# Cached attention on one core: loads by four heads of a batch, K transposes on both sides of the scores, first q by three or four batch pairs

## The chip, the cores and the metric

The kernel runs on one core of a Trainium2 chip. The metric is the device time of one execution in microseconds (us). Before the change it is 869.04 us, the median of three runs (866.92 to 869.71).

## The reference

Two independent attention blocks, A and B, are computed and put side by side in the output. Each has 16 batches of 64 queries, 32 heads of 128 columns and a cache of 512 keys. All data are bf16.

```
q      = (x @ wq), split into heads            # x [16,64,640], wq [640,4096]
scores = q . k_cache * 128**-0.5               # [16,32,64,512]
p      = softmax(scores)
o      = p . v_cache                           # caches [16,32,512,128]
out    = o, heads joined, @ wo                 # wo [4096,640]
return concatenate([a, b], axis=-1)            # [16,64,1280]
```

The caches of both blocks together are 268 MB and are read once.

## The kernel before

**Tiles.** Two batches (a batch pair) fill the 128 rows of a tile: 64 queries of each. A step is one head of one batch pair: a score tile of 128 x 512, its softmax, its product with V. Two steps (two heads) are a macro step, numbered m; there are 256. Two macro steps, four heads, make a period; there are 128. A pass is one block with one half of the heads (16 heads, 8 batch pairs: 64 macro steps); there are four. Inside a pass the batch pairs follow one another, and the 16 heads within each.

**The work of one period on the tensor engine (PE).**

- KX: K arrives with keys on the partitions and is transposed by PE, 32 transposes of 64 rows for each macro step, into PSUM banks 6 and 7. KE on the vector engine (DVE) copies both banks to a slot of `ktp_ring`.
- SM: q times K transposed, the two batches in two column halves of the array. Four score tiles go to banks 2 to 5.
- MX (DVE) takes the row maximum, EX on the scalar engine (ACT) the exponential with its row sum, RC2 (DVE) the reciprocals of two steps, NM on POOL the division. NM also rearranges the columns of p, since K and V give the keys to partitions in different orders.
- TR2 transposes p on PE into banks 2 and 3, which the first two score tiles have left. TA2 (ACT, even m) and TE2 (DVE, odd m) copy it out. PV2 multiplies by V into bank 1, and OE4 (ACT) copies four heads of o out.
- OP2 multiplies o by the first 512 columns of wo, accumulating over the 16 heads in bank 0. OX does the other 128 columns once for every batch pair (16 matmuls, in bank 4, in one period of four). OVP and OXP keep the first half's sum; OVF and OXF add the second half and ST stores.
- QN computes q one half pass ahead, for one head and four batch pairs (five matmuls of 512 columns), into bank 1; QEN copies it to `qc_ring`. The first half pass has no QN before it: there QJ computes q of four heads for one batch pair, in each of the first 16 periods (20 matmuls of 128 columns), and QEJ copies it to `qj_ring`.

**What sets the order.** Every engine runs a list written out before the launch. The templates `PE_T`, `ACT_T`, `DVE_T`, `POOL_T` (lines 39 to 49) give, for a period, each operation, its offset in macro steps, and a time within 6.3 us; sorting by time gives the list. One template holds for the whole run. Dependences become semaphore waits, and redundant ones are pruned.

**Loads.** All loads are issued by SP, in one queue, in the order that `build_plan` computes: a load is due `LEAD` (K, V) or `WLEAD` (weights, x) macro steps before its first use, 9 in both cases, or when its ring slot comes free if that is later. A running clock `t_now`, advanced by `DMA_US` for each load, then ties each load to an instruction of PE: SP waits until PE has got there (`paced`). `STEP_US` says how long a macro step is taken to be.

- K: one load of 512 KB for each macro step, two heads of two batches, 2 KB for each partition and batch (line 702). `kn_ring` has 9 slots.
- V: two loads of 256 KB for each macro step, one for each batch, pieces of 1 KB (line 701). `v_ring` has 10 slots.
- wq and wo: 640 KB for four heads (lines 677 and 685).
- x: transposed by the DMA engines on the way in (line 691), four loads for block A (batch pairs 0; 4 to 7; 1; 2 and 3, in this order) and two for block B.

Of the kernel before, what the change touches and what calls it, by code (L numbers as in the profile page):

```python
# [15 lines left out]
class Cfg:  # L16
# [5 lines left out]
    NVB = 10  # L22
    LEAD = 9.0
    WLEAD = 9.0
    NQ = 2
    QLAG = 4
# [12 lines left out]
    PE_T = (("SM", 0, 0, 0.0), ("SM", 0, 1, 0.21), ("SM", 1, 0, 0.43), ("SM", 1, 1, 0.64), ("QJ", 2, 0, 0.72),  # L39
# [3 lines left out]
    ACT_T = (("OE4", -4, 0, 0.43), ("EX", 0, 0, 1.79), ("QEJ", 2, 0, 1.86), ("EX", 1, 0, 2.27), ("EX", 0, 1, 2.83),  # L43
             ("QEN", -2, 0, 3.25), ("TA2", -2, 0, 4.3), ("OVP", -3, 0, 4.75), ("ST", -9, 0, 5.02),
             ("EX", 1, 1, 5.55), ("OXP", -3, 0, 6.08))
    DVE_T = (("RC2", -1, 0, 0.31), ("MX", 0, 0, 1.61), ("MX", 1, 0, 2.12), ("MX", 0, 1, 2.28), ("KE", 2, 0, 2.3),
             ("MX", 1, 1, 2.91), ("RC2", 0, 0, 4.41), ("OVF", -3, 0, 5.09), ("OXF", -3, 0, 5.38),
             ("TE2", -1, 0, 5.72), ("KE", 3, 0, 5.87))
    POOL_T = (("NM", -1, 0, 1.99), ("NM", -1, 1, 4.17), ("NM", 0, 1, 4.44), ("NM", 0, 0, 5.74))
    ACT_TE = (0,)  # L50
    TRB = (0, 1)
    OXB = 2
    KFULL = ()


class Op:
# [3 lines left out]
    def __init__(self, eng, kind, idx, reads=(), writes=(), dur=0.0, ts=None, aux=None):  # L60
        self.eng = eng
        self.kind = kind
        self.idx = idx
        self.reads = tuple(reads)
        self.writes = tuple(writes)
        self.sem = None
        self.count = None
        self.deps = []
        self.waits = []
        self.early = None  # L70
        self.dur = dur
        self.ts = ts
        self.aux = aux
        self.dma = kind in ("LDK", "LDV", "LDX", "LDWQ", "LDWO", "ST")


def build_plan(dims, cfg):
# [41 lines left out]

    vectors = [tuple(QB * n + i for i in range(QB)) for n in range(HH + cfg.QLAG)]  # L120
    qvec, qcell = {}, {}
    for k in range(NPER):
        u, i, hc = k // PPQ, k % PPQ // HG, k % HG
        if k + PPQ < NPER:
            v = vectors.pop(0)
            qvec[k] = v
            for b in range(QB):
                qcell[u + 1, k % PPQ, b] = v[b]
        if u:
            vectors.append(tuple(sorted(qcell[u, G * hc + g, i] for g in range(G))))  # L130

    def qres(g):
        k, u = g // G, g // G // PPQ
        return ("qj", k % cfg.NQ) if u == 0 else ("qc", qcell[u, g % SPB, k % PPQ // HG])

    def trbank(m):
        return cfg.TRB[m % 2]

    def make_op(kind, m, sub, ts):
# [4 lines left out]
        if kind == "KX":  # L144
            return mk("pe", "KX", m, [("kn", m % cfg.NKB), ("ident",)], [("KTB",)], ts)
        if kind == "KE":
            return mk("dve", "KE", m, [], [("KTB",), ("ktp", m % cfg.NKT)], ts)
        if kind in ("MX", "EX", "NM"):
            g = 2 * m + sub
            r = g % cfg.NR  # L150
            if kind == "MX":
                return mk("dve", "MX", g, [], [("SB", g % cfg.NS), ("negmax", r)], ts)
            if kind == "EX":
                return mk("act", "EX", g, [("negmax", r)], [("SB", g % cfg.NS), ("p", g % cfg.NP), ("rowsum", r)], ts)
            return mk("pool", "NM", g, [("p", g % cfg.NP), ("recip", r)], [("pn", g % cfg.NPN)], ts)
        r0, r1 = g0 % cfg.NR, g1 % cfg.NR
        if kind in ("QJ", "QEJ"):
            if k >= PPQ:
                return None
            if kind == "QJ":  # L160
                return mk("pe", kind, k, [("xT", bp), ("wq", qslot(k % HG))], [("QOB",)], ts)
            return mk("act", kind, k, [], [("QOB",), ("qj", k % cfg.NQ)], ts)
        if kind in ("QN", "QEN"):
            if k not in qvec:
                return None
            u = k // PPQ + 1
            if kind == "QN":
                return mk("pe", kind, k, [("xT", u % 2 * QB + b) for b in range(QB)] + [("wq", qslot(k % PPQ // G))],
                          [("QOB",)], ts)
            return mk("act", kind, k, [], [("QOB",)] + [("qc", c_) for c_ in qvec[k]], ts)  # L170
        if kind == "SM":
            return mk("pe", "SM", (m, sub), [qres(2 * m + sub), ("ktp", m % cfg.NKT)], [("SB", (2 * m + sub) % cfg.NS)],
                      ts)
        if kind == "RC2":
            return mk("dve", "RC2", m, [("rowsum", r0), ("rowsum", r1)], [("recip", r0), ("recip", r1)], ts)
        if kind == "TR2":
            return mk("pe", "TR2", m, [("pn", g0 % cfg.NPN), ("pn", g1 % cfg.NPN), ("ident",)], [("SB", trbank(m))],
                      ts)
        if kind in ("TE2", "TA2"):
            if (kind == "TA2") != (m % 2 in cfg.ACT_TE):  # L180
                return None
            return mk("dve" if kind == "TE2" else "act", kind, m, [], [("SB", trbank(m)), ("pT", m % cfg.NT)], ts)
        if kind == "PV2":
            return mk("pe", "PV2", m, [("pT", m % cfg.NT), ("v", m % cfg.NVB)], [("QOB",)], ts)
        if kind == "OE4":
            return mk("act", "OE4", k, [], [("QOB",), ("oT", k % cfg.NO)], ts)
        if kind == "OP2":
            return mk("pe", "OP2", m, [("oT", k % cfg.NO), ("wo", wslot(ps_, h0 // G))], [("OUTB",)], ts)
        if h0 + 2 != SPB:
            return None  # L190
        lo = grp * MPG
        if kind == "OX":
            return mk("pe", "OX", m, [("oT", i % cfg.NO) for i in range(lo // 2, k + 1)]
                      + [("wo", wslot(ps_, i)) for i in range(HG)], [("SB", cfg.OXB)], ts, aux=(lo, m + 1))
        if kind in ("OVP", "OXP") and ps_ % NHALF == 0:
            return mk("act", kind, m, [], [("OUTB",) if kind == "OVP" else ("SB", cfg.OXB), ("outp", bp, kind[1])], ts,
                      aux=grp)
        if kind in ("OVF", "OXF") and ps_ % NHALF == 1:
            return mk("dve", kind, m, [("outp", bp, kind[1])],
                      [("OUTB",) if kind == "OVF" else ("SB", cfg.OXB), ("out_sb", kind[1])], ts, aux=grp)  # L200
# [4 lines left out]
    templates = {"pe": cfg.PE_T, "dve": cfg.DVE_T, "pool": cfg.POOL_T, "act": cfg.ACT_T}  # L205
    at = {}
    for eng, tmpl in templates.items():
        offs = [t[1] for t in tmpl]
        for k in range(-(max(offs) + 1) // 2 - 1, (NMAC - min(offs)) // 2 + 1):
            for kind, off, sub, t in tmpl:  # L210
                m = 2 * k + off
                if 0 <= m < NMAC:
                    op = make_op(kind, m, sub, 2 * k + 2 * t / cfg.PERIOD)
                    if op is not None:
                        progs[eng].append(op)
                        at[kind, m, sub] = op.ts

# [4 lines left out]
    NEG = -10 ** 9  # L222

    def add(ready, first, lead, rank, kind, idx, writes, aux):
        loads.append((max(ready, first - lead), first, rank,
                      mk("sp", kind, idx, [], writes, first - 0.01, aux=aux)))

    for ps_ in range(NPASS):
        for j in range(HG):
            first = at["QJ", j * MPC, 0] if ps_ == 0 else at["QN", (2 * ps_ - 1) * MPQ + j * MPG, 0]  # L230
            ready = NEG
            if ps_ == 1:
                ready = max(at["QN", j * MPG + MPG - 2, 0], at["QJ", MPQ - MPG + j * MPC, 0])
            elif ps_ > 1:
                ready = at["QN", (2 * ps_ - 2) * MPQ + j * MPG + MPG - 2, 0]
            add(ready, first, cfg.WLEAD, 0, "LDWQ", (ps_, j), [("wq", qslot(j))], (ps_, j))
            i = ps_ * HG + j
            ready = NEG
            if i >= cfg.NWO:
                ready = at["OX", ((i - cfg.NWO) // HG + 1) * MPP - 1, 0]  # L240
            first = at["OP2", ps_ * MPP + j * MPC, 0]
            add(ready, first, cfg.WLEAD, 3, "LDWO", (ps_, j), [("wo", wslot(ps_, j))], (ps_, j))

    for blk in range(NBLK):
        for lo, hi in ((0, 1), (4, 8), (1, 2), (2, 4)) if blk == 0 else ((0, 4), (4, 8)):
            q0 = lo // QB
            if blk:
                first = at["QN", (4 * blk + q0 - 1) * MPQ, 0]
                ready = at["QN", (4 * blk + q0 - 2) * MPQ - 2, 0]
            else:  # L250
                first = at["QN", 0, 0] if q0 else at["QJ", lo * MPG, 0]
                ready = NEG
            add(ready, first, cfg.WLEAD, -1, "LDX", (blk, lo), [("xT", bp) for bp in range(lo, hi)], (blk, lo, hi))

    for m in range(NMAC):
        for kind, ring, n_ring, cons, tb in (("LDK", "kn", cfg.NKB, "KX", 1), ("LDV", "v", cfg.NVB, "PV2", 2)):
            ready = at[cons, m - n_ring, 0] if m >= n_ring else NEG
# [546 lines left out]
```

## Time and profile before

| | us |
|---|---|
| median of three runs | 869.04 |
| profiled execution, its own time | 869.67 |
| its span, first to last instruction | 867.9 |
| PE busy | 832.1 |
| DVE busy | 730.7 |
| ACT busy | 638.0 |
| POOL busy | 418.7 |

The granted clock of the tensor engine is 0.998. The core read 289.41 MB and wrote 2.62 MB. Matmuls overlap in the pipeline, so their durations add to more than the time they take; the distance from one start to the next is the better measure. PEld is PE's weight load, which runs beside its matmuls. A wait marked `<-issue` has no semaphore behind it in the profile. [...]

### The profile page before, as it was taken

How to read it: one execution, taken by the hardware profiler on the slowest of the kernel's cores; microseconds unless marked ns; L12 is line 12 of the kernel's file. 1: busy time of each engine (PE TensorE's matmuls, PEld its weight loads, DVE VectorE, ACT ScalarE, POOL GpSimd, SP SyncE). 2: the span in 40 equal slices, each digit the busy share in tenths (PEclk: the TensorE clock that was granted, in tenths of full speed). 3: DMA queues.
4: the chain of work that ended last, by engine and by line, in shares of the span. 5: the costliest groups of instructions: out<-in, count | busy, mean ns of one | idle time of the engine just before them, and what ended most of it. 6: DMA issues, size and time to landing. Idle time of an engine off the chain costs nothing.

```text
span 867.9 us, 39100 instructions
## 1 busy us (share of the span) xinstructions
PE 832.1 (96%) x17264; PEld 574.4 (66%) x17264; DVE 730.7 (84%) x1184; ACT 638.0 (74%) x1497; POOL 418.7 (48%) x518
## 2 busy tenths in 40 slices
PE   4899999999999999999999999999999999999997
PEld 3567777666666666666666666666766666666664
DVE  4667778888888899898898888888888988999995
ACT  2567777777777777778777777778778777787674
POOL 1344445544554554554455454454555545555553
PEclk9999999999999999999999999999999999999999
DMA  9999999999999999999999999999999999999960
GB/s 257 331 337 327 336 360 366 365 366 359 361 368 367 365 359 305 371 371 369 363 323 369 371 367 365 352 368 364 364 352 355 367 364 342 341 350 370 370 226 17
DMA packets 240746, 297.20 MB, mean 342 GB/s; under 512 B 23488, under 2 KB 175040, under 8 KB 240576
## 3 DMA queue, kind: packets, MB, share of 16 engines
q1 hardware_dynamic: 238272, 292.08, 99.8%
q8 instruction: 135, 2.21, 1.1%
q10 hardware_dynamic: 2304, 2.62, 0.8%
q14 instruction: 35, 0.29, 0.1%
HBM read 289.41 MB, written 2.62 MB: 336 GB/s over the span
## 4 chain that ended last, share of the span: by engine, by line
PE 84%; DMA 6%; ACT 3%; DVE 3%; issue 2%; SPq 2%; ACTq 0%
PE ps L484 15%; PE ps L606 15%; PE ps L546 13%; PE ps L512 13%; PE ps L621 12%; PE ps L584 12%; DMA v_ring<-in_A_v_cache_dram 4%; PE ps L631 3%; ACT p_ring L561 3%; PE ps L497 2%; DVE negmax L555 2%; SPq L691 1%; DMA wo_sb<-in_B_wo_dram 1%; DVE ktp_ring L489 1%; DMA wq_sb<-in_A_wq_dram 1%
## 5 line engine op out<-in xcount | busy, mean ns | idle before, releaser
L575 POOL TENSOR_SCALAR pn_ring<-p_ring,recip 128x512 bf16<-128x512 bf16 x512 | 418.0, 846 | 439.9 <-DVE recip L567 374.1
L561 ACT ACTIVATE p_ring<-ps,negmax 128x512 bf16<-128x512 f32 x512 | 348.8, 687 | 73.8 <-DVE negmax L555 71.1
L555 DVE TENSOR_REDUCE negmax<-ps 128x1 f32<-128x512 f32 x512 | 328.7, 684 | 18.0 <-PE ps L546 11.0
L489 DVE COPY ktp_ring<-ps 128x2048 bf16<-128x2048 bf16 x256 | 311.3, 1216 | 23.7 <-PE ps L484 23.5
L484 PEld LDWEIGHTS ps<-ident,kn_ring 64*128 64x128 bf16 x8192 | 135.4, 95 | 70.0 <-issue 51.9
L584 PEld LDWEIGHTS ps<-ident,pn_ring 128*128 128x128 bf16 x2048 | 132.5, 98 | 66.0 <-ACT p_ring L561 15.4
L484 PE MATMUL ps<-ident,kn_ring 64*128 64x64 bf16 x8192 | 167.5, 191 | 7.0 <-issue 3.9
L613 ACT ACTIVATE oT_ring<-ps 128x512 bf16<-128x512 f32 x128 | 76.4, 597 | 123.0 <-PE ps L606 123.0
L584 PE MATMUL ps<-ident,pn_ring 128*128 128x128 bf16 x2048 | 157.8, 219 | 6.3 <-ACT p_ring L561 3.8
L591 DVE COPY pT_ring<-ps 128x1024 bf16<-128x1024 bf16 x128 | 88.5, 692 | 86.8 <-PE ps L584 86.8
L621 PE MATMUL ps<-wo_sb,oT_ring 128*128 128x512 bf16 x512 | 153.7, 382 | 2.3 <-ACT oT_ring L613 1.4
L606 PE MATMUL ps<-pT_ring,v_ring 128*128 128x64 bf16 x4096 | 145.4, 194 | 7.8 <-DMA v_ring<-in_A_v_cache_dram 4.9
L512 PE MATMUL ps<-xT_sb,wq_sb 128*128 128x512 bf16 x560 | 139.2, 379 | 0.7 <-issue 0.6
L606 PEld LDWEIGHTS ps<-pT_ring,v_ring 128*128 128x128 bf16 x4096 | 128.1, 98 | 16.5 <-DMA v_ring<-in_A_v_cache_dram 5.8
L596 ACT ACTIVATE pT_ring<-ps 128x1024 bf16<-128x1024 bf16 x128 | 131.1, 1024 | 3.1 <-PE ps L584 3.1
L546 PE MATMUL ps<-ktp_ring,qc_ring 128*64 128x512 bf16 x896 | 120.6, 386 | 0.2 <-issue 0.2
L561 ACT ACTIVATION_READ_ACCUMULATOR p_ring<-ps,negmax 128x1 f32 x512 | 104.1, 203 | 0.0
L512 PEld LDWEIGHTS ps<-xT_sb,wq_sb 128*128 128x128 bf16 x560 | 54.7, 98 | 66.8 <-issue 1.0
L525 ACT ACTIVATE qc_ring<-ps 128x256 bf16<-128x256 f32 (+1 forms) x168 | 70.3, 453 | 11.0 <-PE ps L512 9.9
L546 PEld LDWEIGHTS ps<-ktp_ring,qc_ring 128*64 128x64 bf16 x896 | 40.0, 108 | 32.6 <-DVE ktp_ring L489 23.6
L621 PEld LDWEIGHTS ps<-wo_sb,oT_ring 128*128 128x128 bf16 x512 | 34.3, 98 | 10.1 <-ACT oT_ring L613 2.0
L567 DVE RECIPROCAL recip<-rowsum 128x2 f32<-128x2 f32 x256 | 39.7, 155 | 0.5 <-ACT p_ring L561 0.5
(18 smaller groups left out, 172.9 us busy)
## 6 DMA issues: line engine op xcount, KB each, us to landing
kn_ring<-in_A_k_cache_dram SPq DMA_DIRECT2D x128, 512.0 KB, 7.3
v_ring<-in_A_v_cache_dram SPq DMA_DIRECT2D x256, 256.0 KB, 5.8
kn_ring<-in_B_k_cache_dram SPq DMA_DIRECT2D x128, 512.0 KB, 7.2
v_ring<-in_B_v_cache_dram SPq DMA_DIRECT2D x256, 256.0 KB, 5.6
wq_sb<-in_A_wq_dram SPq DMA_DIRECT2D x8, 640.0 KB, 7.9
wo_sb<-in_A_wo_dram SPq DMA_DIRECT2D x8, 640.0 KB, 6.8
wq_sb<-in_B_wq_dram SPq DMA_DIRECT2D x8, 640.0 KB, 8.0
wo_sb<-in_B_wo_dram SPq DMA_DIRECT2D x8, 640.0 KB, 7.9
```

The source lines that it names most:

```text
L484: last = e.transpose(kt_ps[hs][:, j, 64 * t8:64 * t8 + 64], kt[r], ident[r, 64 * hs:64 * hs + 64])
L489: ins = e.tensor_copy(ktp_ring[:, op.idx % NKT], kt_all)
L512: ins = e.matmul(qo_ps, wq_sb[:, qslot(hh // G), kt, (hh % G) * DH:(hh % G + 1) * DH], xT_sb[:, kt, b0 * 128:(b0 + QB) * 128], start=(kt = ...
L546: ins = e.matmul(s_bank(g)[64 * j:64 * j + 64, :], q[:, 64 * j:64 * j + 64], kt[j], start=True, stop=True, tile_position=(0, 64 * j))
L555: ins = e.reduce_max(negmax[:, r:r + 1], s_bank(g), axis=AX.X, negate=True)
L561: ins = e.activation(p_ring[:, g % NP, :], s_bank(g), ACTF.Exp, bias=negmax[:, r:r + 1], scale=1.0, accum_out=rowsum[:, r:r + 1])
L575: ins = e.tensor_scalar(dst, src, recip[:, r:r + 1], 1.0, ALU.mult, ALU.mult)
L584: ins = e.transpose(pt_flat(m)[:, (4 * sub + t) * 128:(4 * sub + t + 1) * 128], pn_ring[:, g % NPN, t * 128:(t + 1) * 128], ident[:, :])
L591: ins = e.tensor_copy(pT_ring[:, m % NT].rearrange("p s t q -> p (s t q)"), pt_flat(m))
L596: ins = e.activation(pT_ring[:, m % NT].rearrange("p s t q -> p (s t q)"), pt_flat(m), ACTF.Copy)
L606: ins = e.matmul(qo_ps[:, col:col + 64], v_ring[:, m % NVB, j, sub, t * DH:(t + 1) * DH], pT_ring[:, m % NT, sub, t, 64 * j:64 * j + 64], ...
L621: ins = e.matmul(out_ps, oT_ring[:, m // 2 % NO, 2 * (m % 2) + sub, :], wo_sb[:, wslot(ps_, hh // G), hh % G, 0:N0], start=(hh == 0), stop ...
```

## The change

- **K** of a macro-step index m is now four heads of one batch (m even: the first batch of the pair, m odd: the second): one contiguous 512 KB, 4 KB for each partition. PE's transposes keep their number and shape. Both loads of a period are needed before its first SM, and SM reads its 512 keys as 16 runs of 32 columns. NM writes every fourth column where it wrote every second.
- **V** is loaded by four heads of a batch, one load of 512 KB for each m, in a ring of five pairs. PV2 of either macro step of a pair needs both loads. The pieces stay 1 KB.
- **KX on both sides.** The even KX of the next period stays behind SM. The odd KX belongs to the period after the next, at the end of the period; its KE comes at the start of the following one. `ktp_ring` has three slots: one for even m, two for odd.
- **q of the first half pass.** QJ is left in the first period alone (four heads, batch pair 0). QZ computes heads 0 to 3 for batch pairs 1 to 3 and heads 4 to 15 for all four pairs, 16 groups of five matmuls within the first three periods, into banks 0 and 1 by turns. All q goes to `qc_ring`, now 64 blocks, and is written in place of q already used, so QEN is one instruction where it was sometimes two. QN moves from offset -2 to -6, two periods later.
- **x of block B** is no longer transposed by DMA: LDXR loads a batch pair as it is, XT transposes it on PE (five transposes of 128 columns into bank 4) in eight periods, XTE (ACT) copies it to `xT_sb`. x of block A comes in three transposing loads (pair 0; pairs 1 to 3; pairs 4 to 7).
- **Order and pace.** Four templates (`PHASES`) replace one, for periods 0 to 15, 16 to 111, 112 to 125, and the last two. OP2 of offset -4 moves behind the first TR2, or in the last template both OP2 behind PV2. `LEAD` is 4.04 macro steps and `WLEAD` 3.9, instead of 9; the second V load of a pair has one macro step less. The planned pace is 34.05 us a macro step for the first 8, 10.93 up to 32, then 3.13.

The diff, cut:

```diff
-    NVB = 10
-    LEAD = 9.0
-    WLEAD = 9.0
-    STEP_US = (3.7, 3.2)
-    DMA_US = dict(LDK=1.38, LDV=1.46, LDWQ=1.8, LDWO=1.8, LDX=1.3)
-    START_US = -16.0
-    BEFORE = 1.5
-    NKT = 2
+    NVP = 5
+    LEAD = 4.04
+    WLEAD = 3.9
+    STEP_US = ((8, 34.05), (32, 10.93), (256, 3.13))
+    DMA_US = dict(LDK=1.36, LDV=1.44, LDWQ=1.8, LDWO=1.8, LDX=1.3, LDXR=0.5)
+    START_US = -93.47
+    BEFORE = 0.6
+    NKT = 3
...
+        (16,
+         (("SM", 0, 0, 0.0), ("SM", 0, 1, 0.21), ("SM", 1, 0, 0.43), ("SM", 1, 1, 0.64), ("KX", 2, 0, 1.14),
+          ("QN", -6, 0, 2.16), ("TR2", -2, 0, 2.49), ("OP2", -4, 0, 3.27), ("OP2", -3, 0, 3.78), ("OX", -3, 0, 3.98),
+          ("TR2", -1, 0, 4.0), ("XT", 0, 0, 4.03), ("KX", 5, 0, 4.57), ("PV2", -2, 0, 5.54), ("PV2", -1, 0, 5.79)),
...
+    def first_q(k, i):
+        return (i, 1, QB, i % 2) if k == 0 and i < G else (G * (k + 1) + i % G, 0, QB, i % 2 if k < 2 else 1)
+
+    def ktslot(m):
+        return m % cfg.NKT if cfg.NKT != 3 else 0 if m % 2 == 0 else 1 + m // 2 % 2
+
+    def x_of(k):
+        u, b = (k - HG) // PPQ + 2, (k - HG) % PPQ // HG
+        if k % HG or u < 4 or u >= NPER // PPQ or u % 4 > 1:
+            return None
+        return u // 4, u % 2 * QB + b
...
         def em_KX(e, op):
...
+            for t in range(16):
+                for hs in range(2):
+                    r = slice(64 * hs, 64 * hs + 64)
+                    last = e.transpose(kt_ps[hs][:, 64 * t:64 * t + 64], kn_ring[r, m % NKB, t * DH:(t + 1) * DH],
+                                       ident[r, 64 * hs:64 * hs + 64])
...
         def em_SM(e, op):
...
+                kt = ktp_ring[:, ktslot(m // 2 * 2 + j)].rearrange("p (hs t h s) -> p hs t h s", hs=2, t=16, h=2)
                 ins = e.matmul(s_bank(g)[64 * j:64 * j + 64, :], q[:, 64 * j:64 * j + 64],
-                               kt[j], start=True, stop=True, tile_position=(0, 64 * j))
+                               kt[:, hd // 2, :, hd % 2, :], start=True, stop=True, tile_position=(0, 64 * j))
...
         def em_NM(e, op):
-            src = p_ring[:, g % NP, :].rearrange("q (th tl pp) -> q th tl pp", th=2, tl=4)
-            dst = pn_ring[:, g % NPN, :].rearrange("q (tl pp th) -> q th tl pp", tl=4, th=2)
+            src = p_ring[:, g % NP, :].rearrange("q (th tl pp) -> q th tl pp", th=4, tl=4)
+            dst = pn_ring[:, g % NPN, :].rearrange("q (tl pp th) -> q th tl pp", tl=4, th=4)
...
         def em_LDKV(e, op):
-            blk, bp, grp, ps_, hh0 = step_info(2 * m)
+            blk, bp, grp, ps_, hh0 = step_info(2 * (m - m % 2))
             h0 = (ps_ % NHALF) * HH + hh0
-            src = blocks[blk][2 if op.kind == "LDV" else 1][2 * bp:2 * bp + 2, h0:h0 + 2]
+            src = blocks[blk][2 if op.kind == "LDV" else 1][2 * bp + m % 2, h0:h0 + G]
             if op.kind == "LDV":
-                vs = src.rearrange("j g (p t) d -> j p g (t d)", p=128)
-                return tuple(e.dma_start(v_ring[:, m % NVB, j], vs[j]) for j in range(2))
-            ins = e.dma_start(kn_ring[:, m % NKB], src.rearrange("j hs (p t) d -> (hs p) j (t d)", t=8))
+                ins = e.dma_start(v_ring[:, m // 2 % NVP, m % 2], src.rearrange("g (p t) d -> p g (t d)", p=128))
+            else:
+                ins = e.dma_start(kn_ring[:, m % NKB], src.rearrange("h (p t) d -> (h p) (t d)", t=16))
+            return ins, ins
+
+        def em_XT(e, op):
+            for kt in range(KT):
+                last = e.transpose(ps[:, cfg.OXB, :].bitcast(BF16)[:, 128 * kt:128 * kt + 128],
+                                   xr_ring[:, bp % cfg.NXR, 128 * kt:128 * kt + 128], ident[:, :])
```

More of the change, by code (lines that the diff above doesn't have):

```diff
@@ L21 @@
     NWO = 6
[L22 to L31 removed]
+    NVP = 5
[6 more added lines that the diff above has]
+    NKT = 3
+    NXR = 2
     NP = 4
@@ L156, in make_op @@
+            return mk("pool" if kind == "NM" else "dve", kind, g, [("p", g % cfg.NP), ("recip", r)], [("pn", g % cfg.NPN)], ts)
         r0, r1 = g0 % cfg.NR, g1 % cfg.NR
         if kind in ("QJ", "QEJ"):
-            if k >= PPQ:
+            if k:
                 return None
             if kind == "QJ":
[L161 to L170, printed above, removed]
+                return mk("pe", kind, 0, [("xT", 0), ("wq", 0)], [bank(1)], ts, aux=[(i, 0, 1) for i in range(G)])
@@ L183, in make_op @@
[L183 to L188, printed above, removed]
+            return mk("dve" if kind == "TE2" else "act", kind, m, [], [bank(cfg.TRB[m % 2]), ("pT", m % cfg.NT)], ts)
+        if kind == "PV2":
+            return mk("pe", "PV2", m, [("pT", m % cfg.NT), ("v", k % cfg.NVP, 0), ("v", k % cfg.NVP, 1)], [bank(1)], ts)
@@ L236, in build_plan @@
             add(ready, first, cfg.WLEAD, 0, "LDWQ", (ps_, j), [("wq", qslot(j))], (ps_, j))
             i = ps_ * HG + j
-            ready = NEG
+            ready = []
             if i >= cfg.NWO:
[L240 to L253, printed above, removed]
@@ new lines, in em_Q, with em_QE @@
+                    first = first or last
+                col += n
+            return first, last
+        def em_QE(e, op):
+            cells = op.aux
+            src = ps[:, op.writes[0][1], :]
+            n = len(cells)
+            if len({b - a for a, b in zip(cells, cells[1:])}) > 1:
+                n = 2
+            first = last = None
+            for i in range(0, len(cells), n):
+                c = cells[i:i + n]
+                last = e.activation(qc_ring[:, c[0]:c[-1] + 1:c[1] - c[0], :],
+                                    src[:, i * 128:(i + n) * 128].rearrange("p (b q) -> p b q", b=n), ACTF.Copy,
+                                    scale=scale)
+                first = first or last
```

307 lines of the change are left out of this document (167 added, 140 removed), and 37 rows, old and new, of tables (PE_T, PHASES).

## The prediction

> **What bounds the kernel now.** I read the page's busy shares first, then DMA and the chain, then cut the span at the first score matmul of periods 0, 16, 112 and 127. A period is two macro steps: four score tiles, two K transposes, two PV products. There are 128.
>
> ```profile
> span 867.9 us, 39100 instructions
> PE 832.1 (96%) x17264; PEld 574.4 (66%) x17264; DVE 730.7 (84%) x1184; ACT 638.0 (74%) x1497; POOL 418.7 (48%) x518
> GB/s 257 331 337 327 336 360 366 365 366 359 361 368 367 365 359 305 371 371 369 363 323 369 371 367 365 352 368 364 364 352 355 367 364 342 341 350 370 370 226 17
> q1 hardware_dynamic: 238272, 292.08, 99.8%
> PE 84%; DMA 6%; ACT 3%; DVE 3%; issue 2%; SPq 2%; ACTq 0%
> ```
>
> PE is full, and so is the load queue. Which of the two sets the pace differs by stage. The windows (us; busy PE, PEld, DVE, ACT, POOL; clock; DMA share; GB/s):
>
> ```profile
> 0.00:12.50 12.50, 3.81 (x84) 3.45 (x84) 1.22 (x1) 1.88 (x2) 0.69 (x6) 1.00 0.77 247
> 12.50:138.90 126.40, 117.92 (x2359) 84.34 (x2351) 90.92 (x143) 86.60 (x193) 50.55 (x62) 0.99 1.04 335
> 138.90:764.00 625.10, 616.59 (x12773) 423.19 (x12770) 547.63 (x887) 477.88 (x1137) 313.67 (x384) 1.00 1.06 359
> 764.00:852.20 88.20, 84.04 (x1931) 57.30 (x1929) 85.46 (x144) 65.10 (x152) 48.59 (x60) 1.00 0.90 307
> 852.20:867.90 15.70, 9.69 (x135) 6.13 (x132) 5.48 (x12) 6.52 (x13) 5.24 (x7) 1.00 0.07 23
> ```
>
> In the third window 96 periods take 625.1 us, 6.51 each, with PE nearly solid. PE's own timeline of one period that contains the 16 matmuls of L631:
>
> ```profile
> 251.59 1.05 PE L546 MATMUL ps<-ktp_ring,qc_ring 128*64 128x512 bf16 x8
> 252.58 0.64 PE L484 MATMUL ps<-ident,kn_ring 64*128 64x64 bf16 x32
> 253.15 0.61 PE L621 MATMUL ps<-wo_sb,oT_ring 128*128 128x512 bf16 x2
> 253.59 1.24 PE L512 MATMUL ps<-xT_sb,wq_sb 128*128 128x512 bf16 x5
> 254.67 0.61 PE L584 MATMUL ps<-ident,pn_ring 128*128 128x128 bf16 x8
> 255.12 0.59 PE L621 MATMUL ps<-wo_sb,oT_ring 128*128 128x512 bf16 x2
> 255.55 1.06 PE L631 MATMUL ps<-wo_sb,oT_ring 128*128 128x128 bf16 x16
> 256.44 0.61 PE L584 MATMUL ps<-ident,pn_ring 128*128 128x128 bf16 x8
> 256.99 0.64 PE L484 MATMUL ps<-ident,kn_ring 64*128 64x64 bf16 x32
> 257.56 1.11 PE L606 MATMUL ps<-pT_ring,v_ring 128*128 128x64 bf16 x32
> ```
>
> Start to start: SM 0.99, each KX 0.57, QN 1.08, OX 0.89, PV 1.04 (ends overlap, so busy times add to more). The next SM starts at 258.60, so 7.01; without OX 6.11; OX comes in one period of four. PE's floor with QN is therefore 6.11 + 0.9/4 = 6.335, without QN 5.255. The third window's floor is 96 x 6.335 = 608.2: only 17 us above PE's own work is there to gain. Nearly all of it is stalls inside a group with no semaphore behind them, the longest this one, and small waits for the K eviction or for OE4:
>
> ```profile
> 208.54 0.26 PE L484 MATMUL ps<-ident,kn_ring 64*128 64x64 bf16 x6 [1.07 <-issue]
> ```
>
> The fourth window has almost no QN, yet its plain period is 5.57, not 5.03: the second P transpose waits there for the third exponential of its period.
>
> ```profile
> 790.83 0.62 PE L584 MATMUL ps<-ident,pn_ring 128*128 128x128 bf16 x8 [0.29 <-ACT p_ring L561]
> ```
>
> **The change, part by part.**
>
> *Start to period 16 (138.9 us now).* Removed: QJ in 16 periods, 20 matmuls of 128 columns each, 1.22 us start to start: 19.6 us. Added: one QJ (1.2), four QZ over 3 batch pairs (five matmuls of 384 columns: three quarters of QN's 1.08, 0.81 each), twelve over 4 pairs (1.08): 1.2 + 3.2 + 13.0 = 17.4. QN starts two periods later (offset -6, not -2). PE's floor from first SM to period 16 is 16 x 5.03 + 13 QN x 1.08 + 16.2 QZ + about 3.1 for OX = 113.8; 12.5 before it gives 126.3. The first SM is taken at 12.5 again, bounds 12 and 14: the first wq goes out behind one K load (it lands at 7.3 now), and QJ, KX and KE lie behind it.
>
> DMA must keep up. Median packet times in the trace are 46 ns for 1 KB, 85 for 2 KB, 55 for 1280 B; 256 B pieces of the x transposes mean 34 at the start. The 4 KB packet is not shown. By the line through 46 and 85 it takes 163; bounds 154 (from 1 KB to 1280 B, 256 B more cost 9 ns, so 36 a KB) and 170 (two of 2 KB). I take 163. Over 16 engines a K load is 128 x 163/16 = 1.30 us (now 1.36), V 1.49, wq 1.86, wo 1.76. Until period 4 PE needs 11 K, 7 V, four wq, three wo and all x (5120 packets, 10.9): 14.3 + 10.4 + 7.4 + 5.3 + 10.9 = 48.3, plus about 2.5 until data flow: 51, against PE's 50 (12.5 + 3 x 5.03 + 16.2 + 6.1). So q work and loads run side by side, where now PE starves (47.9 at period 4, most q still undone). The three-pair x transpose stands ahead of K2 and the second wq on SP, and such an issue held SP for 8.1 us now (four pairs, at 11.1); QZ waits for it and everything behind QZ on PE waits too. For this I add 2 to 4. Period 4 at 54, then 12 periods at 6.335: **130, gain 9**; bounds 126.3 (DMA never late) and 137 (10 us late).
>
> *Middle, 96 periods.* Same matmuls, same count of changes between array shapes. Moves: the odd KX runs a period ahead into its own ktp slot, so SM(1) no longer waits 0.15 for its KE (2.5 us summed). The even KX now waits for KE of the odd; that eviction lies under PV (1.04) and SM (0.99), 1.22 of DVE's time beside 2.03, behind TE2 0.69, so it is just covered; without cover up to 0.15 returns. OP2(-4) goes behind TR2, off the OE4 wait. I take 5 us of the 17 gone, bounds 0 and 17. QEN becomes one ACTIVATE of 597 ns where 56 were two of 381: 9 us of ACT, which idles anyway. In front of QEN nothing new queues.
>
> XT: eight times five transposes of 128 columns; L584's eight take 0.45, so 0.28 each, 2.2 in all, full-array shape next to TR2, and XTE (0.6 to 1.0 by the ACT rows of 512 and 1024 columns) before SM(1,0) needs the bank back. I take 3, bounds 2 and 7. The two B transposes leave SP and DMA (landing 9.6 us; wo behind them landed 8.6 late on the chain); their cover is the lead, so PE gains nothing. Middle 625.1 - 5 = **620** before XT's share is settled: 608.2 + 9 + 3.
>
> Not shown: SM now reads its keys in runs of 32 columns. PV's 64-column matmuls take 32.4 ns where 64 of a 512-column stream take 27: a fresh piece costs 5.5 ns at most there. Upper bound 64 runs x 5.5 = 0.35 a period, lower 0; a gain is excluded, since the columns are the same. I take 0, as the stream within one instruction is the nearest. NM writes every fourth column instead of every second: now 846 ns; four of them would have to pass 1.39 each to fill even the 5.57 period. Taken as 846, bounds 846 and 1390, both hidden by POOL's 440 us of idle.
>
> *End.* Periods 112 to 126: the third-exponential loop stays (order EX(0,0), (1,0), (0,1) is kept), two more QN at 0.54 above 5.57: 88.2 + 1.1 = 89.3. Tail: TR2 of the last steps stands ahead of OP2 and its OE4 wait (0.69 twice): 15.7 - 1 = 14.7.
>
> *Sum:* 130 + 620.2 + 89.3 + 14.7 = 854.2 span. The profiled run took 869.67 with span 867.9, so 1.8 lies around it: 856.0. The median of the three runs, 869.04, is 0.6 under the profiled one: **855.4**.
>
> **Rivals.** *Starved by the shorter lead (slower).* Loads go out 4.04 macro steps ahead instead of 9: 12.8 us before use at 3.17 a step, the second V of a pair 9.6. Now a K load is issued some 25 us before its KX and lands 17 us before it. Landing takes 7.3 us now, under a queue of 2.6 MB; V, now 512 KB, should land like K. That leaves 5.5 and 2.3 us. Four wo loads at each pass start add 7 us of DMA; in the trace the slack fell from 18 to 10 at pass 2. It decides when landing exceeds 9.6. A dip of 8 us against 2.3 of slack stops PE for 5.7 at each of three pass starts, 17 in all, and a start as late as its bound (137) adds 7: 855.4 + 24 = 880. Against it: removing the transposes thins that dip, and K and V alone need 2.1 MB, 5.65 us at the 371 GB/s of slices 17 and 18, beside PE's 6.335.
>
> The Trainium skill, "DMA: Bandwidth & Descriptors", Specifications, puts HBM's share of one core at about 358 GB/s. By that rule the 2.26 MB of a period would take 6.32, no spare would exist, and this rival would hold at 880; my sum by the measured rate stays 855. The trace's 371 GB/s in whole slices is above the rule, so the measurement decides.
>
> *SM slowed by its short runs:* 0.35 x 112 = 39: 894. Nothing in the trace speaks for it. *No change:* period 16 at 137, the stalls unchanged, XT paid: 867.9 - 2 + 3 + 1.2: 870. The early GB/s (327 to 337 with x in the queue) speak for a slow start, the 17 us of q work beside loads against. *More:* DMA never late (126.3) and a thinner queue ends the issue stalls: 126.3 + 608.2 + 2.2 + 89.3 + 14.7 = 840.7, time 842.
>
> **Numbers.** Forecast (845 to 866) 0.65, more 0.11, no change 0.07, starved 0.13, short runs 0.04. About 0.3% (2.6 us) is what a measurement can tell. Faster 0.76, same 0.07, slower 0.17. Range 841 to 872: it leaves out most of the slower cases and a little below; the forecast's own range is 845 to 866.
>
> **What would show it.** First SM near 12.5; L546 of period 16 near 130, of period 112 near 750; middle periods 6.11 and 7.01 without 6.26; x of B gone from the transposes; kn landing in 5 to 7 us. Wrong if v_ring or kn_ring waits of PE sum to over 15 us after 140 us, if SM's eight take over 1.05, if period 4 starts after 60, or if NM passes 1.3 us.

## The result and the profile after

The changed kernel takes 880.51 us (median of four runs, 879.49 to 884.78) against 869.38 for the kernel before beside it: ratio 1.0135, 95% interval 1.0087 to 1.0183. It is slower. The forecast was 855.4, faster.

The page of the changed kernel: span, busy time by engine, GB/s in 40 slices, the load queue, and the chain that ended last.

```profile
span 879.4 us, 38528 instructions
PE 838.5 (95%) x17084; PEld 563.2 (64%) x17084; DVE 729.0 (83%) x1184; ACT 644.3 (73%) x1450; POOL 665.0 (76%) x518
GB/s 269 333 376 372 333 340 332 354 349 343 361 346 318 314 366 341 338 348 363 358 358 368 322 355 334 329 353 342 356 345 347 361 352 357 333 340 350 363 307 92
q1 hardware_dynamic: 197344, 292.06, 96.8%
PE 57%; POOL 23%; DMA 9%; DVE 8%; issue 2%; SPq 0%; ACT 0%; POOLq 0%
```

POOL is the new entry: 665.0 us busy where it was 418.7, and 23% of a chain in which it did not appear at all. PE's busy time, 838.5 against 832.1, is up too; with the same 17084 matmuls and a mended NM it is 827.8 (the permuted exponential, below), so some 10 us of it look like matmuls that are held, not work.

The same cuts as before (first SM of periods 0, 16, 112 and 127; columns: busy PE, PEld, DVE, ACT, POOL, clock, DMA share, GB/s). DMA share adds up the time of all packets over 16 engines' time, and the packets of the load queue by themselves already add to 1.04 in the middle of the kernel before, so a share above 1 needs no second queue.

```profile
0.00:15.60 15.60, 5.27 (x116) 4.71 (x116) 2.45 (x2) 1.88 (x2) 0.69 (x6) 1.00 0.94 224
15.60:129.10 113.50, 112.04 (x2127) 73.17 (x2125) 89.56 (x144) 84.39 (x192) 82.05 (x62) 1.00 1.04 352
129.10:770.40 641.30, 625.30 (x12811) 419.80 (x12810) 546.04 (x886) 483.91 (x1090) 496.44 (x385) 1.00 1.00 346
770.40:862.20 91.80, 84.99 (x1910) 58.27 (x1907) 85.83 (x143) 66.86 (x151) 77.98 (x61) 1.00 0.97 330
862.20:879.40 17.20, 10.86 (x135) 7.24 (x132) 5.14 (x11) 7.26 (x15) 7.87 (x7) 0.90 0.23 79
```

| stage, us | before | forecast | after |
|---|---|---|---|
| to period 16 | 138.9 | 130 | 129.1 |
| periods 16 to 111 | 625.1 | 620.2 | 641.3 |
| periods 112 to 126 | 88.2 | 89.3 | 91.8 |
| tail | 15.7 | 14.7 | 17.2 |
| span | 867.9 | 854.2 | 879.4 |

Stage times, here and below, are those of each kernel's profiled execution, which lies up to 4 us from its median. The start gained what it should. The middle lost 16 us instead of gaining 5, and both later stages lost some. The plain period of the middle (no OX in it), 6.11 at its best before, is 6.40 in its median now. The costliest group of the page, and who waits for it in the list of waits (us in total, times, longest):

```profile
L635 POOL TENSOR_SCALAR pn_ring<-p_ring,recip 128x512 bf16<-128x512 bf16 x512 | 664.3, 1420 | 205.4 <-DVE recip L627 185.5
```

```profile
PEld ps L681 <- POOL pn_ring L635: 52.3, 80, 1.4
PEld ps L666 <- DMA v_ring<-in_A_v_cache_dram: 4.7, 5, 2.6
PEld ps L666 <- DMA v_ring<-in_B_v_cache_dram: 4.4, 8, 1.0
```

NM takes 1420 ns where it took 846. Back to back, two take 2.65 us and four 5.17. The wait shows on L681 because the last OP2 matmul in front of TR2 carries TR2's wait. The period from 398.54 shows the order of it, first PE, then DVE, then POOL:

```profile
398.54 1.05 PE L596 MATMUL ps<-ktp_ring,qc_ring 128*64 128x512 bf16 x8
399.52 0.64 PE L549 MATMUL ps<-ident,kn_ring 64*128 64x64 bf16 x32
...
401.63 1.31 PE L681 MATMUL ps<-wo_sb,oT_ring 128*128 128x512 bf16 x4
402.78 0.61 PE L644 MATMUL ps<-ident,pn_ring 128*128 128x128 bf16 x8
```

```profile
397.64 1.22 DVE L556 COPY ktp_ring<-ps 128x2048 bf16<-128x2048 bf16 x1
398.99 0.69 DVE L605 TENSOR_REDUCE negmax<-ps 128x1 f32<-128x512 f32 x1
399.59 0.16 DVE L627 RECIPROCAL recip<-rowsum 128x2 f32<-128x2 f32 x1
```

```profile
399.85 5.17 POOL L635 TENSOR_SCALAR pn_ring<-p_ring,recip 128x512 bf16<-128x512 bf16 x4 [1.23 <-DVE recip L627]
```

RC2 of the previous macro step stands behind the first MX, 1.05 us after the period's first SM. This move is in the templates of periods 16 to 111 and of the last two only; the description of the change does not list it. In the kernel before RC2 stood ahead of MX, at 251.82 in the period from 251.59: 0.23 after.

```profile
251.82 0.15 DVE L567 RECIPROCAL recip<-rowsum 128x2 f32<-128x2 f32 x1
252.04 1.89 DVE L555 TENSOR_REDUCE negmax<-ps 128x1 f32<-128x512 f32 x3
```

```profile
252.07 1.63 POOL L575 TENSOR_SCALAR pn_ring<-p_ring,recip 128x512 bf16<-128x512 bf16 x2 [0.65 <-DVE recip L567]
```

In the changed kernel NM starts on the later RC2, two of them take 2.65 us, and the second TR2, 4.24 us into the period, has to wait. At 846 ns the pair would have been done a microsecond earlier.

Two theories remained. **NM:** the longer NM, together with its later start, is the loss. **Lead:** the shorter lead starves PE of loads, the rival of the prediction whose price, 880, is the time that was measured.

### The profile page after: what moved, and what is told of

Its sections match the earlier page's. It is cut to its first block, busy times and chain, and to the rows that moved or that the text cites. A ratio compares the mean times of both kernels' runs of the same rounds, so it can differ in the third digit from the quotient of the medians.

```text
span 879.4 us, 38528 instructions
## 1 busy us (share of the span) xinstructions
PE 838.5 (95%) x17084; PEld 563.2 (64%) x17084; DVE 729.0 (83%) x1184; ACT 644.3 (73%) x1450; POOL 665.0 (76%) x518
## 4 chain that ended last, share of the span: by engine, by line
PE 57%; POOL 23%; DMA 9%; DVE 8%; issue 2%; SPq 0%; ACT 0%; POOLq 0%
POOL pn_ring L635 23%; PE ps L666 14%; PE ps L549 10%; PE ps L596 8%; PE ps L644 8%; PE ps L681 7%; PE ps L566 7%; DVE negmax L605 6%; DMA v_ring<-in_B_v_cache_dram 5%; DMA v_ring<-in_A_v_cache_dram 3%; PE ps L691 3%; DVE ktp_ring L556 1%; DMA wq_sb<-in_A_wq_dram 1%; DVE recip L627 1%; PE ps L774 0%
## 5 line engine op out<-in xcount | busy, mean ns | idle before, releaser
L635 POOL TENSOR_SCALAR pn_ring<-p_ring,recip 128x512 bf16<-128x512 bf16 x512 | 664.3, 1420 | 205.4 <-DVE recip L627 185.5
L605 DVE TENSOR_REDUCE negmax<-ps 128x1 f32<-128x512 f32 x512 | 333.4, 679 | 24.1 <-PE ps L596 12.9
L566 PE MATMUL ps<-xT_sb,wq_sb 128*128 128x512 bf16 (+2 forms) x660 | 160.4, 377 | 5.3 <-DMA wq_sb<-in_A_wq_dram 4.3
L681 PE MATMUL ps<-wo_sb,oT_ring 128*128 128x512 bf16 x512 | 150.3, 382 | 14.9 <-POOL pn_ring L635 7.2
L644 PEld LDWEIGHTS ps<-ident,pn_ring 128*128 128x128 bf16 x2048 | 133.1, 98 | 48.5 <-ACT p_ring L621 5.6
L644 PE MATMUL ps<-ident,pn_ring 128*128 128x128 bf16 x2048 | 156.8, 219 | 2.2 <-POOL pn_ring L635 2.1
L666 PE MATMUL ps<-pT_ring,v_ring 128*128 128x64 bf16 x4096 | 143.3, 194 | 8.3 <-DMA v_ring<-in_A_v_cache_dram 4.1
L596 PE MATMUL ps<-ktp_ring,qc_ring 128*64 128x512 bf16 x1024 | 136.8, 389 | 0.2 <-ACT p_ring L621 0.2
L656 ACT ACTIVATE pT_ring<-ps 128x1024 bf16<-128x1024 bf16 x128 | 131.0, 1024 | 0.3 <-PE ps L644 0.3
L681 PEld LDWEIGHTS ps<-wo_sb,oT_ring 128*128 128x128 bf16 x512 | 42.6, 98 | 69.4 <-POOL pn_ring L635 52.3
L582 ACT ACTIVATE qc_ring<-ps 128x512 bf16<-128x512 f32 (+1 forms) x129 | 75.7, 587 | 15.1 <-PE ps L566 14.9
L596 PEld LDWEIGHTS ps<-ktp_ring,qc_ring 128*64 128x64 bf16 x1024 | 47.3, 110 | 34.0 <-issue 1.0
```

The costliest lines, as they stand in the source:

```text
L566: last = e.matmul(dst[:, col:col + n], wq_sb[:, qslot(hh // G), kt, (hh % G) * DH:(hh % G + 1) * DH], xT_sb[:, kt, lo * 128:hi * 128], sta ...
L596: ins = e.matmul(s_bank(g)[64 * j:64 * j + 64, :], q[:, 64 * j:64 * j + 64], kt[:, hd // 2, :, hd % 2, :], start=True, stop=True, tile_pos ...
L605: ins = e.reduce_max(negmax[:, r:r + 1], s_bank(g), axis=AX.X, negate=True)
L635: ins = e.tensor_scalar(dst, src, recip[:, r:r + 1], 1.0, ALU.mult, ALU.mult)
L644: ins = e.transpose(pt_flat(m)[:, (4 * sub + t) * 128:(4 * sub + t + 1) * 128], pn_ring[:, g % NPN, t * 128:(t + 1) * 128], ident[:, :])
L656: ins = e.activation(pT_ring[:, m % NT].rearrange("p s t q -> p (s t q)"), pt_flat(m), ACTF.Copy)
```

## Experiments

Ratios are against the kernel before in the same runs (867 to 874 us throughout).

### What NM costs by the way it writes

```diff
+            if g % 4 == 0:
+                ins = e.activation(p_ring[:, g % NP, :].rearrange("q (tl pp th) -> q tl pp th", tl=4, th=4),
+                                   s_bank(g).rearrange("q (th tl pp) -> q tl pp th", th=4, tl=4), ACTF.Exp,
+                                   bias=negmax[:, r:r + 1], scale=1.0, accum_out=rowsum[:, r:r + 1])
...
+            pr, pn = p_ring[:, g % NP, :], pn_ring[:, g % NPN, :]
+            if g % 4 == 0:
+                ins = e.tensor_scalar(pn, pr, recip[:, r:r + 1], 1.0, ALU.mult, ALU.mult)
+            elif g % 4 == 1:
+                src = pr.rearrange("q (th tl pp) -> q th tl pp", th=4, tl=4)
+                dst = pn.rearrange("q (tl th pp) -> q th tl pp", tl=4, th=4)
...
+            elif g % 4 == 2:
+                src = pr.rearrange("q (th tl pp) -> q th tl pp", th=2, tl=4)
+                dst = pn.rearrange("q (tl pp th) -> q th tl pp", tl=4, th=2)
...
+            else:
+                src = pr.rearrange("q (th tl pp) -> q th tl pp", th=4, tl=4)
+                dst = pn.rearrange("q (tl pp th) -> q th tl pp", tl=4, th=4)
```

> The changed kernel with four forms of NM, by step number modulo 4: 0 writes the columns in one contiguous run (the exponential of these steps reads its score bank in permuted order instead, so the keys still match V), 1 writes runs of 32 contiguous columns, 2 writes every second column in runs of 64 as the kernel before, 3 every fourth column in runs of 32 as the changed kernel. Forms 1 and 2 leave the keys out of V's order, which changes the output and not the amount of work. If the 8-byte distance between written elements makes NM slow: forms 0 and 1 cost 846 ns or less, form 2 about 846, form 3 about 1420. If the number of runs makes it slow: form 1 costs about as much as form 3, form 2 about 846, form 0 least. The permuted exponential costs 687 ns if the scalar engine reads a bank in any order at one rate; over 900 if the order matters.

Form 0 writes one contiguous run, form 1 runs of 32 columns, form 2 every second column, form 3 every fourth, as the changed kernel does. The groups of that run; L640, L644, L648 and L652 are forms 0 to 3, L622 the permuted exponential, L626 the plain one. This kernel was run once and took 859.17 us:

```profile
L640 POOL TENSOR_SCALAR pn_ring<-p_ring,recip 128x512 bf16<-128x512 bf16 x128 | 88.9, 695 | 49.7 <-DVE recip L632 48.0 <-PE ps L661 1.7
L644 POOL TENSOR_SCALAR pn_ring<-p_ring,recip 128x512 bf16<-128x512 bf16 x128 | 89.1, 696 | 40.7 <-PE ps L661 21.9 <-DVE recip L632 18.8
L648 POOL TENSOR_SCALAR pn_ring<-p_ring,recip 128x512 bf16<-128x512 bf16 x128 | 107.7, 841 | 299.7 <-DVE recip L632 299.7
L652 POOL TENSOR_SCALAR pn_ring<-p_ring,recip 128x512 bf16<-128x512 bf16 x128 | 181.2, 1416 | 2.9 <-DVE recip L632 2.9
L622 ACT ACTIVATE p_ring<-ps,negmax 128x512 bf16<-128x512 f32 x128 | 88.0, 687 | 74.2 <-DVE negmax L605 74.2
L626 ACT ACTIVATE p_ring<-ps,negmax 128x512 bf16<-128x512 f32 x384 | 262.7, 689 | 1.4 <-DVE negmax L605 1.3
```

Sixteen runs of 32 cost as much as one run of 512, so it is not the number of runs. It is the distance between written elements: 695 ns at 2 bytes, 841 at 4, 1416 at 8. The scalar engine reads a bank in this permuted order in 687 ns, in the plain order in 689, so this reorder is free there. The Trainium skill, "GPSIMD Engine Reference", Performance pitfalls for Q7 kernels, puts a rise of half at reads whose step exceeds 8 bytes. The trace has a rise of 68% between 4 and 8 bytes, for writes, at 8 already; that section does not speak of writes.

### The changed kernel with the NM of the kernel before

```diff
-            src = p_ring[:, g % NP, :].rearrange("q (th tl pp) -> q th tl pp", th=4, tl=4)
-            dst = pn_ring[:, g % NPN, :].rearrange("q (tl pp th) -> q th tl pp", tl=4, th=4)
+            src = p_ring[:, g % NP, :].rearrange("q (th tl pp) -> q th tl pp", th=2, tl=4)
+            dst = pn_ring[:, g % NPN, :].rearrange("q (tl pp th) -> q th tl pp", tl=4, th=2)
```

> The changed kernel, with NM writing every second column as the kernel before does; the keys then do not match V's order, the amount of work is the same. Theory (NM on POOL became the slow link of the softmax chain): NM back to about 846 ns, plain periods of the middle 6.40 to 6.11, middle 641 to about 620, last stretch 91.8 to about 89; total about 880.5 - 21 - 3 = 856, ratio to the kernel before 0.985. Rival (the shorter lead starves PE of K and V): the total stays at 875 or more, ratio above 1.005, and the waits of PE for v_ring stay at 8 us or grow.

Measured: 857.47 us, ratio 0.9869 (0.9839 to 0.9900); NM 845 ns. Stages: 130.7, 626.8, 87.6, 14.4; plain middle period 6.11. The one write distance is worth 23 us and turns a loss into a gain. The waits for v_ring are still there, and somewhat larger (NM first, then the waits):

```profile
L635 POOL TENSOR_SCALAR pn_ring<-p_ring,recip 128x512 bf16<-128x512 bf16 x512 | 417.7, 845 | 433.1 <-DVE recip L627 399.5
```

```profile
PE ps L666 <- DMA v_ring<-in_A_v_cache_dram: 6.6, 4, 2.0
PE ps L666 <- DMA v_ring<-in_B_v_cache_dram: 5.7, 7, 1.5
```

So the lead does cost something, but it is not what made the changed kernel slower.

### The changed kernel with the old lead

```diff
-    LEAD = 4.04
-    WLEAD = 3.9
+    LEAD = 9.0
+    WLEAD = 9.0
```

> The changed kernel with LEAD and WLEAD of 9 macro steps again. Theory (NM): only the waits of PE for v_ring in the middle go, 8.6 us, so about 872, ratio 1.003; plain periods stay at 6.40. Rival (shorter lead): the 16 us lost in the middle come back, 860 or less, ratio 0.99.

Measured: 878.47, ratio 1.0108 (1.0077 to 1.0138); plain middle period 6.39. The middle gains 10 us (631.3), the waits for v_ring are gone from the list, but period 16 comes at 136.0, 7 us later. The total barely moves and misses the 872 of the NM theory, because the loss at the start was not foreseen; the plain period stays at 6.39, as that theory had it. What the short lead costs in the middle it earns at the start.

### The kernel before with the slow NM

```diff
-            src = p_ring[:, g % NP, :].rearrange("q (th tl pp) -> q th tl pp", th=2, tl=4)
-            dst = pn_ring[:, g % NPN, :].rearrange("q (tl pp th) -> q th tl pp", tl=4, th=2)
+            src = p_ring[:, g % NP, :].rearrange("q (th tl pp) -> q th tl pp", th=4, tl=4)
+            dst = pn_ring[:, g % NPN, :].rearrange("q (tl pp th) -> q th tl pp", tl=4, th=4)
```

> The kernel before with one thing of the change: NM writes every fourth column (keys then do not match V's order, the work is the same). Theory (NM): NM takes about 1420 ns here too, the plain middle period grows from 6.11 to about 6.4 and the last stretch too, so 96 x 0.2 to 0.3 plus some 5: 890 to 903, ratio 1.025 to 1.04. Rival (the NM is hidden, other parts of the change cost the time): 869, ratio within 1.003.

Measured: 874.25, ratio 1.0057 (1.0034 to 1.0080); NM 1417 ns; stages 140.1, 624.9, 90.1, 16.9. The middle did not move at all (625.1), and the total lies outside what either theory said. A slow NM costs nothing there in the old order, and 1.9 and 1.2 us in the last stage and the tail. So the 1420 ns alone are not the cause of the middle's loss either.

```profile
L575 POOL TENSOR_SCALAR pn_ring<-p_ring,recip 128x512 bf16<-128x512 bf16 x512 | 668.5, 1417 | 194.8 <-DVE recip L567 150.5
```

### RC2 in its old place

In the template of periods 16 to 111, one time of `DVE` changes and with it one place in the order:

```diff
-         (("KE", 3, 0, 0.42), ("MX", 0, 0, 0.59), ("RC2", -1, 0, 0.65), ("MX", 0, 1, 0.86), ("MX", 1, 0, 1.17),
+         (("KE", 3, 0, 0.42), ("MX", 0, 0, 0.59), ("RC2", -1, 0, 0.5), ("MX", 0, 1, 0.86), ("MX", 1, 0, 1.17),
```

> The changed kernel with one place moved: in the template of periods 16 to 111, RC2 of the last macro step stands ahead of MX of the first score tile, not behind it; NM stays at 1420 ns. Theory (a slow NM is only felt because RC2, and so NM, starts 1.05 us after the first SM): NM's pair ends about 0.7 us earlier, plain middle periods go from 6.40 to 6.11 and the middle from 641 to about 622; the last stretch, another template, keeps its 91.8; total about 861, ratio 0.99. Rival (POOL is full at four NM of 1.3 to 1.4 us a period, wherever they start): 878 or more, ratio above 1.007.

Measured: 865.31, ratio 0.9948 (0.9926 to 0.9970); NM still 1421 ns; plain middle period 6.11, middle 623.8, last stage unchanged at 91.8. The total is 4 us above the 861 expected. A period of that run by the timeline, DVE and POOL (one with OX); its first SM is at 395.14; the last line is the group of all NM:

```profile
395.36 0.16 DVE L627 RECIPROCAL recip<-rowsum 128x2 f32<-128x2 f32 x1
395.59 1.89 DVE L605 TENSOR_REDUCE negmax<-ps 128x1 f32<-128x512 f32 x3
```

```profile
395.61 2.65 POOL L635 TENSOR_SCALAR pn_ring<-p_ring,recip 128x512 bf16<-128x512 bf16 x2 [0.46 <-DVE recip L627]
```

```profile
L635 POOL TENSOR_SCALAR pn_ring<-p_ring,recip 128x512 bf16<-128x512 bf16 x512 | 681.3, 1421 | 169.9 <-DVE recip L627 145.2
```

NM begins 0.47 us after the first SM instead of 1.31, and the slow pair fits. POOL still does four slow NM a period and is not full. The loss in the middle is therefore the product of two edits, the NM write and the place of RC2; either alone is hidden there.

The last stage is another matter. It keeps its 4 us (91.8 against 87.6 with NM at 845 ns), and in the template of periods 112 to 125 RC2 stands ahead of the first MX already. There the slow NM is enough by itself: four take 5.2 us of a plain period of 5.57, and PE waits 6.1 us for them in that stage of the changed kernel. What RC2's place costs in the last two periods was not tried.

### The order mended where it is free

```diff
-            ins = e.activation(p_ring[:, g % NP, :], s_bank(g), ACTF.Exp, bias=negmax[:, r:r + 1], scale=1.0,
-                               accum_out=rowsum[:, r:r + 1])
+            ins = e.activation(p_ring[:, g % NP, :].rearrange("q (tl pp th) -> q tl pp th", tl=4, th=4),
+                               s_bank(g).rearrange("q (th tl pp) -> q tl pp th", th=4, tl=4), ACTF.Exp,
+                               bias=negmax[:, r:r + 1], scale=1.0, accum_out=rowsum[:, r:r + 1])
...
-            ins = e.tensor_scalar(dst, src, recip[:, r:r + 1], 1.0, ALU.mult, ALU.mult)
+            ins = e.tensor_scalar(pn_ring[:, g % NPN, :], p_ring[:, g % NP, :], recip[:, r:r + 1], 1.0, ALU.mult, ALU.mult)
```

> The changed kernel with the key order mended elsewhere: EX reads its score bank in V's order (687 ns in the probe, as before) and NM writes one contiguous run (695 ns in the probe). Everything is computed. Theory (NM's write distance is what cost the time): plain middle periods 6.11, middle about 626 as with the two-column NM, last stretch 87 to 88; total 855 to 858, ratio 0.985. Rival (the write order of NM mattered only through something else, such as TR2 reading pn): not under 865.

Measured: 858.68, ratio 0.9864 (0.9818 to 0.9910); NM 696 ns; stages 131.0, 627.4, 87.6, 14.4. With everything computed, the changed kernel comes within 3.3 us of the forecast 855.4. The stages say that this is in part luck: the middle is 7 us above its forecast.

The same in the kernel before, with its own order of the columns; NM becomes the contiguous one of the diff above:

```diff
-            ins = e.activation(p_ring[:, g % NP, :], s_bank(g), ACTF.Exp, bias=negmax[:, r:r + 1], scale=1.0,
-                               accum_out=rowsum[:, r:r + 1])
+            ins = e.activation(p_ring[:, g % NP, :].rearrange("q (tl pp th) -> q tl pp th", tl=4, th=2),
+                               s_bank(g).rearrange("q (th tl pp) -> q tl pp th", th=2, tl=4), ACTF.Exp,
+                               bias=negmax[:, r:r + 1], scale=1.0, accum_out=rowsum[:, r:r + 1])
```

> The kernel before, with its own key order made by EX reading the score bank permuted, and NM writing one contiguous run (695 instead of 846 ns). Everything is computed. Theory (in the order of the kernel before, NM is off the path at 846 ns; only far above that is it felt): 869, ratio within 0.004 of 1. Rival (each nanosecond of NM is on the path): 96 x 4 x 0.15 us and more, 58 us, under 820; or a part of that, under 864.

Measured: 869.42, ratio 0.9998 (0.9985 to 1.0011), NM 692 ns. In the old order NM is hidden from 692 to 846 ns, and up to 1417 but for 5 us, none of them in the middle.

### What the lead is worth

The kernel before, with the short lead alone:

```diff
-    LEAD = 9.0
-    WLEAD = 9.0
+    LEAD = 4.04
+    WLEAD = 3.9
```

> The kernel before, with LEAD 4.04 and WLEAD 3.9 alone. If the short lead starves PE by itself: waits for v_ring and kn_ring in the middle, 10 to 20 us there, 878 or more. If it costs only what the changed kernel showed with it (8.6 us of waits) and helps the start: 866 to 874.

Measured: 890.14, ratio 1.0247 (1.0204 to 1.0290), the middle 644.7. Here the rival of the prediction is real: PE waits for V, wo and K.

```profile
PE ps L606 <- DMA v_ring<-in_B_v_cache_dram: 8.2, 10, 1.7
PE ps L621 <- DMA wo_sb<-in_B_wo_dram: 7.7, 5, 2.5
PE ps L606 <- DMA v_ring<-in_A_v_cache_dram: 3.8, 5, 1.2
PE ps L621 <- DMA wo_sb<-in_A_wo_dram: 3.3, 5, 1.0
PE ps L484 <- DMA kn_ring<-in_B_k_cache_dram: 2.6, 5, 1.1
```

Most of it falls in periods 65 to 76, which took 6.7 to 11.7 us each: the start of block B with its x transposes and wo loads. The pace (`STEP_US`, `START_US`) stayed as it was set for the lead of 9. The changed kernel has taken the transposes of B away; that its lead of four steps holds better there fits, but was not tried apart.

The kernel of the permuted exponential with a longer lead for K and V from macro step 40 on:

```diff
+        lead = cfg.LEAD if m < 40 else 8.0
```

> The kernel of the permuted exponential, with LEAD 8 for K and V from macro step 40 on and 4.04 before it. Theory (with NM out of the way, the short lead costs what is left above PE's floor in the middle: 12 us of waits for v_ring): those waits go, middle about 616, start as with the short lead (129 to 131), total 846 to 850. Rival (the lead does not matter once the loads are not behind): 855 or more.

Measured: 882.24, ratio 1.0154 (1.0111 to 1.0197): 24 us worse than without, the opposite of what was expected. Periods 17 to 37 took up to 12.1 us, and PE waits for the weights:

```profile
PE ps L550 <- DMA wq_sb<-in_A_wq_dram: 7.7, 3, 3.4
PE ps L681 <- DMA wo_sb<-in_A_wo_dram: 7.6, 5, 3.6
PE ps L666 <- DMA v_ring<-in_A_v_cache_dram: 6.8, 4, 2.6
```

All loads share one queue. The order of the code says that the jump puts four steps of K and V ahead of nearer loads, and that weights, which kept the short lead, come behind them; which of the two cost more was not tried. From period 80 to 111 the same kernel ran at 6.37 a period, near PE's floor of 6.335, but the short lead gave 6.41 there too. So the lead was let grow slowly, for all loads alike:

```diff
         t = at[first]
+        lead += min(4.0, 0.05 * max(0.0, t - 36.0))
```

> The kernel of the permuted exponential, with the lead of all loads, weights included, growing from macro step 36 on by a twentieth of a step a step up to 4 steps more. Theory (the sudden LEAD 8 of K and V alone put eight loads ahead of nearer ones and left the weights behind; a lead that grows together, out of DMA's spare rate, costs nothing): waits for v_ring and the weights of the middle go, middle 614 to 620 beside 627, start unchanged, total 845 to 852, ratio 0.975. Rival (DMA has no spare rate, so a longer lead only changes which load is late): 857 or more.

Measured: 845.41, ratio 0.9719 (0.9692 to 0.9747). It beats both kernels. The windows at its own cuts:

```profile
15.80:129.30 113.50, 112.16 (x2125) 73.18 (x2125) 89.60 (x144) 84.35 (x192) 42.45 (x63) 1.00 1.04 350
129.30:741.50 612.20, 611.62 (x12811) 425.08 (x12811) 545.90 (x886) 473.26 (x1090) 260.51 (x384) 1.00 1.05 369
741.50:829.10 87.60, 84.56 (x1910) 58.22 (x1908) 84.92 (x143) 65.41 (x151) 40.75 (x60) 1.00 0.90 314
```

The middle is 612.2, 4 us above PE's floor of 608.2 (XT, some 3 us, is in it); PE is busy in 611.6 of it, no wait for a load is left there, and DMA moves 369 GB/s throughout where the changed kernel moved 346.

## Why the prediction was wrong, point by point

- **NM: the step that failed.** It was "taken as 846, bounds 846 and 1390, both hidden by POOL's 440 us of idle". The value is 1420, outside the bounds; "if NM passes 1.3 us" was the prediction's own sign of being wrong. And the cover was misread: POOL's idle total says nothing of when NM may start. Four NM take 5.17 us back to back, so POOL is not full even in the 5.57 period that the 1.39 bound was set by. The prediction laid out the new order of OP2, KX and KE, but not that RC2 moves behind MX, and so did not see that NM's chain (EX, RC2, NM, TR2) lost 0.8 us of slack in the same edit. With the same kernel and NM at 845 ns the time is 857.5; with NM slow and RC2 in its old place 865.3, the rest being the last stage and the tail.
- **Start.** 130 forecast, 129.1 measured. The first SM came at 15.6, not 12.5 to 14: wq landed at 10.0 behind one K load and x, and the third KX has to wait 1.3 us for KE. Period 4 at 51.6 instead of 54 made up for it, so the match is in part luck: the x transpose did hold SP for 7.6 us, but PE had QZ work left and waited for no load between the first wq and period 16. From there periods 4 to 15 take 77.5 us where they took 91.0; 12 times the 1.22 of QJ is 14.6.
- **Middle without NM.** 620 forecast, 627 with the NM mended. The waits for V (12 us in the list with the two-column NM, 11 with the permuted exponential), which the forecast set to nothing with the lead taken as enough, cover the missing 7; without them, in the last run, the middle is 612.2. The sum slips too: 5 of 17 gone and 3 for XT make 623.2, while 620.2 has 8 gone. That the wait of SM for KE went, and the OE4 wait with it, fits the plain periods: 50 of 72 within 0.05 of the 6.11 floor in the kernel of the permuted exponential, 34 before; neither was tried alone.
- **The rival "starved by the shorter lead" at 880** hit the time and not the cause. Undoing the lead gave back 10 us in the middle and lost 7 at the start. But its dips are real, and they come where it put them: in the kernel of the permuted exponential the runs of slow periods are 36 to 40, 68 to 71 and 100 to 102, not far behind the pass starts at 32, 64 and 96, and the growing lead removes them. What the lead does cost is the 15 us between the middles of 627.4 and 612.2 (13 between the medians), near the 17 that the rival set.
- **The load rate.** The prediction weighed the 358 GB/s that the Trainium skill, "DMA: Bandwidth & Descriptors", Specifications, gives as HBM's share of one core, and set it aside. Rightly: the last run held 369 GB/s over 612 us, with one core running. The Trainium skill, "HBM Reference", Specifications (TRN2), says that a core which streams alone gets more than that share, and the trace agrees.
- **SM's short runs** cost nothing: 0.99 us from SM to the next group in the median, as before. **XT**: 0.38 from its five transposes to the next group, eight times, so 3.0 us. The prediction had 0.28 each and took 3 in all, which is most of the 4 us that the best run has above the floor.
- **4 KB packets**: median 159 ns in the trace's packet records, 163 assumed (the 2 KB median is 86, not 85, and the line would then give 166); the mean of the changed kernel is 178, against 2 x 90, so the packets of K got hardly faster (1%).
- **A reading.** The wo load that "landed 8.6 late on the chain" took 8.57 us there as a piece of the chain; PE waited 0.2 us for it.
- **End.** 89.3 forecast, 87.6 with NM mended, 91.8 with it slow; tail 14.7 forecast, 14.4 and 17.2.

## What to carry to other kernels

An engine that is half idle can still set the pace, if its work lies in a chain between two engines that have no slack: read when the operation may start and when its result is due, not its share of the span. Where a layout forces a reorder, put it into an instruction whose time does not change with the order (here the exponential reading PSUM), and measure each candidate's access pattern once in a probe, in one run. When a shared load queue needs a longer lead, try it for all loads together and growing slowly: that gained 13 us here, where a jump for K and V alone lost 24.

## What the hardware showed that was not expected

- POOL's TENSOR_SCALAR on 128x512 bf16: 695 ns writing contiguously or in runs of 32, 841 with every second column, 1416 with every fourth.
- ACT's exponential over 128x512 from PSUM: 687 to 689 ns in order, 687 ns with a step of 128 columns in the innermost dimension.
- A load stream of mostly 4 KB and 1 KB pieces held 369 GB/s for 612 us beside a PE that was busy 99.9% of that time.
